# Nine first tiles instead of ten, and a matrix product begun one quarter of k at a time

## The chip, the core and the metric

The kernel runs on one core of a Trainium2 chip. The core has a matrix engine (TensorE, PE in the profile), which multiplies a 128-row stationary operand with a moving operand of up to 512 columns and adds into PSUM banks; a vector engine (VectorE, DVE); a scalar engine (ScalarE, ACT); GpSimd (POOL, almost idle here); and a sync engine (SP), which only issues transfers. Sixteen DMA engines move the data; two queues feed them here, that of SP (q1 in the profile) and that of ACT (q10). PSUM has eight banks of 128 x 512 float32.

The metric is the time of one execution on the device in microseconds (us), where lower is better.

## What is computed

A linear layer whose weight is first pruned 2:4: along the input dimension the 1024 rows of `w` form 256 groups of four, and in every group and column the entries survive whose magnitude is at least the second largest of the four.

```python
B, S, D = 16, 512, 1024            # x: (16, 512, 1024), w: (1024, 1024), b: (1024), all bfloat16
wg  = w.reshape(D // 4, 4, D)
mag = jnp.abs(wg)
thr = second largest of the four magnitudes, per group and column
wp  = (wg * (mag >= thr)).reshape(D, D)
out = jnp.einsum("bsd,df->bsf", x, wp) + b
```

Seen as matrices this is 8192 tokens x 1024 inputs times 1024 inputs x 1024 outputs, with a bias.

## The kernel before

**Tiles.** The tokens form 64 tiles of 128. A tile needs 16 matmuls of 512 columns: eight blocks of 128 inputs (k) times two halves h of the outputs. The weight is pruned on the chip, which takes a while, so the tiles fall into two kinds. The last 54 tiles (t = 10 to 63) are the natural ones: their x is transposed by a DMA transpose on SP's queue, in batches of 2, 4, 8, 8, ... tiles, and each runs its 16 matmuls in a row (line 301) from the finished weight `wp_nat`. The first T = 10 tiles are worked off while the weight is still being pruned, one weight piece at a time.

**Weight pieces.** `w` is cut into two row halves g (512 rows each, k half 0 and 1) and eight pieces: (g=0) columns 0:128, 128:256, 256:512, 512:768, 768:1024, and (g=1) 0:256, 256:512, 512:1024. They are numbered 0 to 7. In the loaded layout partition p holds four consecutive rows m = 0..3, that is one pruning group, so that pruning is elementwise between four slices. For g = 0 the first tiles use this layout directly: x's first half is loaded plainly, transposed on PE against an identity matrix with a stride of four (four transposes per tile, line 160) and copied by ACT to `xT` (line 165). For g = 1 the piece is unpacked into natural row order: four SBUF-to-SBUF transfers j = 0..3, each of 32 partitions, into `wp_nat[h][:, 4 + j]` (line 150); x's second half for the first tiles comes as `xg1` by one DMA transpose (line 98). So transfer j delivers exactly the quarter m = j of k that matmul m of a first tile reads.

**The written order.** A string FRONT gives the order of all work of the first tiles. Each engine and each DMA queue runs its own part strictly in that order; between engines only data, PSUM banks and DMA semaphores make anyone wait. The tokens:

- `W`, `w`: warm-up matmuls on zeros, of 512 and 128 columns (PE).
- `A.i`: magnitudes of piece i (DVE for pieces 0 and 2, ACT for the others); `P.i`: the seven DVE operations that prune it.
- `T.t`, `C.t`: the four transposes of tile t on PE, and their copy on ACT.
- `M.i.t`: the four matmuls of tile t with piece i; `X.q.t`: those of tile t with a whole 512-column quadrant q = 2g + h.
- `V.h.t`: the g = 0 sum of half h is copied from its bank to SBUF in float32 (ACT). `O.h.t`: the g = 1 sum is added to that (DVE). `B.h.t`: the bias is added and the half goes to the output tile (DVE), which is stored when both halves are there.
- `U.g.h.c0.c1`: the four unpacking transfers, issued on SP's queue; `Z` the same on ACT's queue, for the g = 0 half that only natural tiles read.
- `L.n`: the DMA transpose of batch n, on SP's queue, behind the `U`s.

PSUM banks are handed out in turn, eight in a circle, at each `T` and at the first matmul of each quadrant of a tile; the next owner waits for the `V`, `O` or final addition that empties the bank. DMA transfers share eight completion semaphores in turn, so that a transfer's issue can also wait for the transfer that used its semaphore before.

After FRONT come the natural tiles. On DVE they carry along the `B` additions that are left over (three per tile, four in the first). Outputs are stored in pairs of tiles on ACT's queue; tile 62 goes alone, and the last tile, 63, is computed in four column parts so that little is left to do after its last matmul.

**Places the change touches.** `T = 10` (line 39), the load of x for tiles 8 and 9 (line 91), `mm_part` (lines 169 to 179), the batch list (line 224), FRONT (lines 231 to 241) and the pairing of stores (lines 306 to 313).

Of the kernel before, what the change touches and what calls it, by code (L numbers as in the profile page):

```python
# [10 lines left out]
def kernel(  # L11
# [7 lines left out]
    nc = tc.nc  # L19
    P = 128  # L20
# [11 lines left out]
    NT = NTOK // P  # L32
    FH = 512
# [2 lines left out]
    xf = x.flatten_outer_dims()  # L36
    of = out.flatten_outer_dims()

    T = 10
    NE = 8  # L40

    const = ctx.enter_context(tc.tile_pool(name="const", bufs=1))
# [18 lines left out]
    pieces = [(0, 0, 128), (0, 128, 256), (0, 256, 512), (0, 512, 768), (0, 768, 1024),  # L61
              (1, 0, 256), (1, 256, 512), (1, 512, 1024)]
# [25 lines left out]
    load_x(4, 6)  # L88
    load_x(6, 8)
    load_w(0, 512, 1024)  # L90
    load_x(8, 10)
    load_w(1, 0, 512)
    load_w(1, 512, 1024)
    bias_sb = const.tile([P, Dout], bf16, name="bias_sb")
# [12 lines left out]
    def warm(n):  # L107
        K(nc.tensor.matmul(bank[7][:, :n], lhsT=zeros[:, :P], rhs=zeros[:, :n], start=True, stop=True))  # L108
# [3 lines left out]
    def abs_piece(i, on_act):  # L112
        g, c0, c1 = pieces[i]
        n = c1 - c0
        if n <= 256:
            mag = mags_pool.tile([P, 4, n], bf16, name="mag")[:]
        else:
            mag = const.tile([P, 4, n], bf16, name=f"mag_{i}")[:]
        if on_act:
            K(nc.scalar.activation(mag, w_of(i), Act.Abs))  # L120
        else:
            K(nc.vector.tensor_single_scalar(
                mag.bitcast(u16), w_of(i).bitcast(u16), 0x7FFF, op=Alu.bitwise_and))
        mags[i] = mag
# [41 lines left out]
        xT[t] = xt  # L166


    def mm_part(q, t, c0, c1):
        g, h = divmod(q, 2)  # L170
        if c0 == 0 and q > 0:
            own[(q, t)] = next_bank()
        dst = bank[own[(q, t)]][:, c0:c1]
        for m in range(4):
            if g == 0:
                lhs, rhs = xT[t][:, m, :], w_gh[(0, h)][:, m, c0:c1]
            else:
                lhs, rhs = xg1[:, m, t * P:(t + 1) * P], wp_nat[h][:, 4 + m, c0:c1]
            K(nc.tensor.matmul(dst, lhsT=lhs, rhs=rhs, start=c0 == 0 and m == 0, stop=c1 == FH and m == 3))  # L179
# [11 lines left out]
    def to_stage(h, t):  # L191
        stage[(h, t)] = const.tile([P, FH], fp32, name=f"stage{h}_{t}")
        K(nc.scalar.copy(stage[(h, t)][:], bank[own[(h, t)]][:]))  # L193
# [20 lines left out]
    def issue_batch(t0, nb):  # L214
# [6 lines left out]
            xN[t0 + j] = xt[:, :, j * P:(j + 1) * P]  # L221


    batches = [(T, 2), (T + 2, 4)] + [(t, 8) for t in range(T + 6, NT, 8)]

# [1 line left out]


    FRONT = """
        A.0 A.1 P.0 W W W W W W W W w w T.0 T.1 C.0 T.2 T.3 C.1 P.1 w M.0.0 C.2 M.0.1 T.4 C.3 T.5 M.0.2 C.4 T.6 T.7
        A.2 M.0.3 C.5 M.0.4 P.2 M.1.0 M.1.1 C.6 M.0.5 M.1.2 C.7 M.0.6 M.1.3 M.1.4 A.3 M.0.7 M.1.5 M.1.6 M.1.7 A.4
        M.2.0 P.3 M.2.1 V.0.0 M.2.2 V.0.1 M.2.3 T.8 T.9 C.8 M.2.4 M.2.5 C.9 P.4 M.2.6 A.5 M.2.7 X.0.8 V.0.2 X.0.9
        V.0.3 V.0.4 M.3.0 P.5 U.1.0.0.256 V.0.5 M.3.1 M.3.2 V.0.6 M.3.3 V.0.7 M.4.0 M.3.4 A.6 M.3.5 M.4.1 V.0.8 P.6
        U.1.0.256.512 M.4.2 V.0.9 M.3.6 M.4.3 A.7 M.3.7 M.4.4 M.4.5 M.4.6 V.1.0 P.7 U.1.1.0.512 L.0 L.1 L.2 M.4.7
        V.1.1 X.1.8 V.1.2 X.1.9 V.1.3 M.5.0 V.1.4 M.5.1 V.1.5 M.5.2 V.1.6 M.5.3 M.6.0 V.1.7 M.5.4 V.1.8 O.0.0 M.5.5
        M.6.1 V.1.9 Z.0.0.0.512 Z.0.1.0.512 B.0.0 M.5.6 O.0.1 M.5.7 M.6.2 B.0.1 M.6.3 M.6.4 O.0.2 M.6.5 O.0.3 M.6.6
        M.6.7 O.0.4 X.2.8 O.0.5 X.2.9 O.0.6 M.7.0 O.0.7 O.0.8 M.7.1 O.0.9 M.7.2 O.1.0 M.7.3 O.1.1 M.7.4 O.1.2 O.1.3
        M.7.5 O.1.4 M.7.6 O.1.5 M.7.7 O.1.6 X.3.8 B.0.2 O.1.7 X.3.9 O.1.8 O.1.9  # L240
    """
    for tok in FRONT.split():
        k, *n = tok.split(".")
        n = [int(c) for c in n]
        if k in "Ww":
            warm(FH if k == "W" else P)
        elif k == "A":
            abs_piece(n[0], n[0] not in (0, 2))
        elif k == "P":
            prep_piece(n[0])  # L250
        elif k == "T":
            transpose_half(n[0])
        elif k == "C":
            copy_half(n[0])
        elif k == "M":
            g, c0, c1 = pieces[n[0]]
            h = c0 // FH
            mm_part(2 * g + h, n[1], c0 - h * FH, c1 - h * FH)
# [32 lines left out]
    for bi, (t0, nb) in enumerate(batches):  # L291
        if bi >= 1 and bi + 2 < len(batches):
            issue_batch(*batches[bi + 2])
        for t in range(t0, t0 + nb):
            if t == NT - 1:
                last_tile(t)
                continue
            bks = (next_bank(), next_bank())
            for kt in range(KT):
                for h in range(2):  # L300
                    K(nc.tensor.matmul(bank[bks[h]][:], lhsT=xN[t][:, kt, :], rhs=wp_nat[h][:, kt, :],  # L301
                                       start=kt == 0, stop=kt == KT - 1))
# [12 lines left out]
_INS = ['x', 'w', 'b']  # L315
_OUTS = [((16, 512, 1024), 'bfloat16')]
# [25 lines left out]
```

## Time and profile before

| | before |
|---|---|
| time, median of 3 runs | 234.63 us (234.07 to 235.2) |
| the profiled execution: its time | 234.52 us |
| its span, first to last instruction | 232.7 us |
| PE busy | 227.3 us (98%) |
| DVE busy | 117.6 us (51%) |
| ACT busy | 22.7 us (10%) |
| granted TensorE clock, mean | 1.000 |
| DMA, mean over the span | 164 GB/s |

The 1.8 us between the profiled execution's time and its span lie before its first and after its last instruction. A matmul's duration in the profile runs from its start to the modelled end of its result and overlaps its successor: a 512-column matmul has 379 ns there, while the next starts 0.216 us after it; for 256 columns the starts are 0.109 us apart, for 128 columns 0.056 us. What a matmul costs PE is the distance between starts. A few matmul records are missing from the trace; the places show as a "wait" of 0.05 us in the chain of waits, every 50 matmuls.

### The profile page before, as it was taken

To read this page: it belongs to the slowest core of one execution; us is meant where nothing else is said; L and a number is where in the kernel's file an instruction comes from. 1 tells how busy PE (TensorE), PEld (TensorE's weight loads), DVE (VectorE), ACT (ScalarE), POOL (GpSimd) and SP (SyncE) were. 2 spreads that over 40 slices of the span, in tenths; PEclk is the share of its full clock that TensorE was granted. 3 is DMA by queue.
4 is the path that set the end of the run, shared out by engine and by line. 5 is a ranking of instruction groups with operands and counts; after the bars stand their busy time and mean duration, and the time that the engine had idled before them with its cause. 6 is when DMAs were issued, how large, how long until landed. Compare 5 with 4: busy or idle time off the path is not lost.

```text
span 232.7 us, 2893 instructions
## 1 busy us (share of the span) xinstructions
PE 227.3 (98%) x1199; PEld 114.8 (49%) x1219; DVE 117.6 (51%) x209; ACT 22.7 (10%) x38; POOL 0.7 (0%) x6
## 2 busy tenths in 40 slices
PE   7999999999999999999999999999999999999995
PEld 3878774444444444444444444444444444444443
DVE  3999898969375244234334334324424423433434
ACT  3989600000000000000000000000000000000000
POOL 1000000000000000000000000000000000000000
PEclk9999999999999999999999999999999999999999
DMA  6996499999989401993229932597228991122222
GB/s 197 350 211 145 98 197 165 229 315 289 213 215 346 152 24 66 262 236 136 90 44 254 205 130 92 112 218 216 88 90 188 158 250 65 64 93 90 90 90 90
DMA packets 76700, 38.19 MB, mean 164 GB/s; under 512 B 61840, under 2 KB 68496, under 8 KB 76688
## 3 DMA queue, kind: packets, MB, share of 16 engines
q1 hardware_dynamic: 66192, 19.86, 47.1%
q10 hardware_dynamic: 10496, 18.16, 22.4%
q8 instruction: 9, 0.15, 0.3%
q14 instruction: 3, 0.02, 0.0%
HBM read 3.67 MB, written 16.78 MB: 88 GB/s over the span
## 4 chain that ended last, share of the span: by engine, by line
PE 95%; DMA 2%; SPq 1%; issue 1%; DVE 0%
PE bank L301 78%; PE bank L179 15%; DMA xh<-in_x_dram 2%; PE bank L276 2%; PE bank L160 1%; SPq L71 0%; SPq L79 0%; DVE o_sb L286 0%
## 5 line engine op out<-in xcount | busy, mean ns | idle before, releaser
L301 PE MATMUL bank<-wp_nat,xTb 128*128 128x512 bf16 x737 | 161.7, 379 | 0.8
L207 DVE TENSOR_TENSOR o_pair<-bank,bias_sb 128x512 bf16<-128x512 f32 x106 | 68.2, 685 | 98.0 <-PE bank L301 93.6
L301 PEld LDWEIGHTS <-xTb 128*128 128x128 bf16 x752 | 73.6, 98 | 88.7
L301 PE MATMUL bank<-wp_nat,xTs 128*128 128x512 bf16 x94 | 20.8, 379 | 0.1
L179 PE MATMUL bank<-w,xT 128*128 128x256 bf16 (+2 forms) x174 | 18.2, 262 | 0.2
L179 PE MATMUL bank<-wp_nat,xg 128*128 128x256 bf16 (+1 forms) x111 | 17.5, 318 | 0.1
L201 DVE TENSOR_TENSOR o_sb<-stage,bias_sb 128x512 bf16<-128x512 f32 x20 | 13.0, 685 | 7.3 <-DMA out_dram<-o_sb 7.2
L179 PEld LDWEIGHTS <-xT 128*128 128x128 bf16 x176 | 14.5, 98 | 3.1 <-ACT xT L165 0.3
L301 PEld LDWEIGHTS <-xTs 128*128 128x128 bf16 x96 | 9.4, 98 | 11.3
L179 PEld LDWEIGHTS <-xg 128*128 128x128 bf16 x112 | 11.0, 98 | 6.4
L197 DVE TENSOR_TENSOR stage<-bank,stage 128x512 f32<-128x512 f32 x20 | 13.0, 684 | 2.0 <-PE bank L179 1.8
L193 ACT COPY stage<-bank 128x512 f32<-128x512 f32 x20 | 10.3, 681 | 0.3 <-PE bank L179 0.3
L120 ACT ACTIVATE mag<-w 128x1024 bf16<-128x1024 bf16 (+2 forms) x6 | 6.9, 1167 | 0.4 <-DMA w<-in_w_dram 0.4
L142 DVE TENSOR_TENSOR mask<-mag,thr 128x1024 bf16<-128x1024 bf16 (+2 forms) x8 | 5.5, 692 | 0.3
L143 DVE TENSOR_TENSOR w<-w,mask 128x1024 bf16<-128x1024 bf16 (+2 forms) x8 | 5.5, 692 | 0.3
L165 ACT COPY xT<-bank 128x512 bf16<-128x512 bf16 x10 | 5.2, 598 | 1.9 <-PE bank L160 1.9
L108 PE MATMUL bank<-zeros 128*128 128x512 bf16 (+1 forms) x11 | 4.0, 536 | 1.2 <-DVE zeros L101 1.2
L276 PE MATMUL bank<-wp_nat,xTb 128*128 128x128 bf16 (+2 forms) x32 | 3.7, 272 | 0.0
L160 PE MATMUL bank<-ident,xh 128*128 128x128 bf16 x40 | 3.1, 228 | 0.3 <-DMA xh<-in_x_dram 0.3
L133 DVE TENSOR_TENSOR hi<-mag 128x512 bf16<-128x512 bf16 (+2 forms) x8 | 3.4, 420 | 0.1
L134 DVE TENSOR_TENSOR lo<-mag 128x512 bf16<-128x512 bf16 (+2 forms) x8 | 3.3, 417 | 0.0
L276 PEld LDWEIGHTS <-xTb 128*128 128x128 bf16 x32 | 2.5, 98 | 1.3
(16 smaller groups left out, 16.0 us busy)
## 6 DMA issues: line engine op xcount, KB each, us to landing
out_dram<-o_pair ACTq DMA_DIRECT2D x26, 512.0 KB, 2.9
out_dram<-o_sb ACTq DMA_DIRECT2D x10, 256.0 KB, 5.3
w<-in_w_dram SPq DMA_DIRECT2D x3, 512.0 KB, 7.0
xh<-in_x_dram SPq DMA_DIRECT2D x4, 256.0 KB, 4.9
wp_nat<-w ACTq DMA_DIRECT2D x8, 128.0 KB, 4.8
wp_nat<-w SPq DMA_DIRECT2D x8, 64.0 KB, 2.1
wp_nat<-w SPq DMA_DIRECT2D x4, 128.0 KB, 4.5
xh<-in_x_dram ACTq DMA_DIRECT2D x1, 256.0 KB, 4.2
```

Source lines behind the costliest of these rows:

```text
L120: K(nc.scalar.activation(mag, w_of(i), Act.Abs))
L142: K(nc.vector.tensor_tensor(mask, mag, thr[:, None, :].to_broadcast([P, 4, n]), op=Alu.is_ge))
L143: K(nc.vector.tensor_tensor(w_of(i), w_of(i), mask, op=Alu.mult))
L160: K(nc.tensor.transpose(dst[:, m, :], xv[:, m, :], ident[:]))
L165: K(nc.scalar.copy(xt[:], src))
L179: K(nc.tensor.matmul(dst, lhsT=lhs, rhs=rhs, start=c0 == 0 and m == 0, stop=c1 == FH and m == 3))
L193: K(nc.scalar.copy(stage[(h, t)][:], bank[own[(h, t)]][:]))
L197: K(nc.vector.tensor_tensor(st, bank[own[(2 + h, t)]][:], st, op=Alu.add))
L201: K(nc.vector.tensor_tensor(get_o(t)[:, f], stage.pop((h, t))[:], bias_sb[:, f], op=Alu.add))
L207: K(nc.vector.tensor_tensor(o_sb[:, f], bank[bk][:], bias_sb[:, f], op=Alu.add))
L276: K(nc.tensor.matmul(bank[bk][:, :c1 - c0], lhsT=xN[t][:, kt, :], rhs=wp_nat[h][:, kt, c0:c1], start=kt == 0, stop=kt == KT - 1))
L301: K(nc.tensor.matmul(bank[bks[h]][:], lhsT=xN[t][:, kt, :], rhs=wp_nat[h][:, kt, :], start=kt == 0, stop=kt == KT - 1))
```

## The change

T becomes nine. Tile 9 loses its transposes, its copy, its four `X` groups and its `V`, `O` and `B`; it becomes the first natural tile, and the batches are now 3, 4, 8, 8, ... tiles. `mm_part` takes the list of k quarters to multiply, and a new token `N.i.t.m` multiplies one quarter m of tile t with piece i. FRONT begins piece 5 with `N.5.0.0 N.5.1.0 N.5.2.0` (quarter 0 of tiles 0, 1, 2), then quarter 1 of these three tiles, and so on; piece 6 begins with the quarters of tile 0, and piece 7 with those of tiles 0 and 1 in turn. Elsewhere FRONT changes its order: near the start `M.0.2` stands before `T.4` instead of behind `T.5`; `T.8` stands after `V.0.0`; all `B`s move behind FRONT. The `Z`s still follow the last `V`, and that is now `V.1.8`. With an odd number of first tiles the pairs of stored tiles shift by one, and tiles 61 and 62 are stored one by one.

```diff
-    T = 10
+    T = 9
...
-    load_x(8, 10)
+    load_x(8, 9)
...
-    def mm_part(q, t, c0, c1):
+    def mm_part(q, t, c0, c1, ms=range(4)):
         g, h = divmod(q, 2)
-        if c0 == 0 and q > 0:
+        if c0 == 0 and q > 0 and 0 in ms:
             own[(q, t)] = next_bank()
         dst = bank[own[(q, t)]][:, c0:c1]
-        for m in range(4):
+        for m in ms:
...
-    batches = [(T, 2), (T + 2, 4)] + [(t, 8) for t in range(T + 6, NT, 8)]
+    batches = [(T, 12 - T), (12, 4)] + [(t, 8) for t in range(16, NT, 8)]
...
-        A.0 A.1 P.0 W W W W W W W W w w T.0 T.1 C.0 T.2 T.3 C.1 P.1 w M.0.0 C.2 M.0.1 T.4 C.3 T.5 M.0.2 C.4 T.6 T.7
-        A.2 M.0.3 C.5 M.0.4 P.2 M.1.0 M.1.1 C.6 M.0.5 M.1.2 C.7 M.0.6 M.1.3 M.1.4 A.3 M.0.7 M.1.5 M.1.6 M.1.7 A.4
-        M.2.0 P.3 M.2.1 V.0.0 M.2.2 V.0.1 M.2.3 T.8 T.9 C.8 M.2.4 M.2.5 C.9 P.4 M.2.6 A.5 M.2.7 X.0.8 V.0.2 X.0.9
-        V.0.3 V.0.4 M.3.0 P.5 U.1.0.0.256 V.0.5 M.3.1 M.3.2 V.0.6 M.3.3 V.0.7 M.4.0 M.3.4 A.6 M.3.5 M.4.1 V.0.8 P.6
-        U.1.0.256.512 M.4.2 V.0.9 M.3.6 M.4.3 A.7 M.3.7 M.4.4 M.4.5 M.4.6 V.1.0 P.7 U.1.1.0.512 L.0 L.1 L.2 M.4.7
-        V.1.1 X.1.8 V.1.2 X.1.9 V.1.3 M.5.0 V.1.4 M.5.1 V.1.5 M.5.2 V.1.6 M.5.3 M.6.0 V.1.7 M.5.4 V.1.8 O.0.0 M.5.5
-        M.6.1 V.1.9 Z.0.0.0.512 Z.0.1.0.512 B.0.0 M.5.6 O.0.1 M.5.7 M.6.2 B.0.1 M.6.3 M.6.4 O.0.2 M.6.5 O.0.3 M.6.6
-        M.6.7 O.0.4 X.2.8 O.0.5 X.2.9 O.0.6 M.7.0 O.0.7 O.0.8 M.7.1 O.0.9 M.7.2 O.1.0 M.7.3 O.1.1 M.7.4 O.1.2 O.1.3
-        M.7.5 O.1.4 M.7.6 O.1.5 M.7.7 O.1.6 X.3.8 B.0.2 O.1.7 X.3.9 O.1.8 O.1.9
+        A.0 A.1 P.0 W W W W W W W W w w T.0 T.1 C.0 T.2 T.3 P.1 C.1 w M.0.0 C.2 M.0.1 C.3 M.0.2 T.4 A.2 T.5 C.4
+        M.0.3 P.2 T.6 T.7 C.5 M.0.4 M.1.0 C.6 M.1.1 M.0.5 M.1.2 C.7 M.0.6 M.1.3 A.3 M.1.4 M.0.7 M.1.5 M.1.6 A.4
+        M.1.7 P.3 M.2.0 M.2.1 V.0.0 M.2.2 A.5 T.8 M.2.3 M.2.4 C.8 M.2.5 V.0.1 P.4 M.2.6 V.0.2 M.2.7 X.0.8 V.0.3
+        V.0.4 M.3.0 M.3.1 V.0.5 M.3.2 P.5 U.1.0.0.256 V.0.6 M.3.3 V.0.7 M.3.4 M.3.5 A.6 M.3.6 M.4.0 V.0.8 M.4.1
+        V.1.0 P.6 U.1.0.256.512 M.3.7 M.4.2 V.1.1 M.4.3 A.7 M.4.4 M.4.5 M.4.6 M.4.7 V.1.2 P.7 U.1.1.0.512 L.0 L.1
+        L.2 X.1.8 V.1.3 N.5.0.0 N.5.1.0 N.5.2.0 N.5.0.1 N.5.1.1 N.5.2.1 N.5.0.2 N.5.1.2 N.5.2.2 N.5.0.3 N.5.1.3
+        N.5.2.3 V.1.4 V.1.5 V.1.6 M.5.3 M.5.4 V.1.7 M.5.5 V.1.8 Z.0.0.0.512 Z.0.1.0.512 M.5.6 N.6.0.0 N.6.0.1 M.5.7
+        N.6.0.2 N.6.0.3 M.6.1 O.0.0 M.6.2 O.0.1 M.6.3 M.6.4 O.0.2 M.6.5 M.6.6 O.0.3 M.6.7 O.0.4 X.2.8 O.0.5 N.7.0.0
+        N.7.1.0 N.7.0.1 N.7.1.1 N.7.0.2 N.7.1.2 N.7.0.3 N.7.1.3 O.0.6 O.0.7 M.7.2 O.0.8 O.1.0 M.7.3 O.1.1 M.7.4
+        O.1.2 M.7.5 O.1.3 M.7.6 O.1.4 O.1.5 M.7.7 O.1.6 X.3.8 O.1.7 O.1.8
...
+        if k in "MN":
+            g, c0, c1 = pieces[n[0]]
+            h = c0 // FH
+            mm_part(2 * g + h, n[1], c0 - h * FH, c1 - h * FH, n[2:] or range(4))
...
-            if j == 1 or t == NT - 2:
-                dst = of[(t - j) * P:(t + 1) * P, :].rearrange("(j p) f -> p j f", p=P)
-                K(nc.scalar.dma_start(dst, o_pair[:, :j + 1, :]))
+            if j == 1 or t >= NT - 3:
+                j0 = j if t >= NT - 3 else 0
+                dst = of[(t - j + j0) * P:(t + 1) * P, :].rearrange("(j p) f -> p j f", p=P)
+                K(nc.scalar.dma_start(dst, o_pair[:, j0:j + 1, :]))
```

More of the change, by code (lines that the diff above doesn't have):

```diff
@@ L244 @@
         n = [int(c) for c in n]
-        if k in "Ww":
+        if k in "MN":
+            g, c0, c1 = pieces[n[0]]
+            h = c0 // FH
+            mm_part(2 * g + h, n[1], c0 - h * FH, c1 - h * FH, n[2:] or range(4))
+        elif k in "Ww":
             warm(FH if k == "W" else P)
@@ L254 @@
             copy_half(n[0])
[L255 to L258, printed above, removed]
         elif k == "X":
```

## The prediction

> **What bounds the kernel now.** I read the page's busy times first, then the chain of work that ended last, then the order of time on PE, DVE, ACT and SP in the first 44 us, and last the transfers of that stretch. The busy times, and the chain (start us, length us, what):
>
> ```profile
> span 232.7 us, 2893 instructions
> PE 227.3 (98%) x1199; PEld 114.8 (49%) x1219; DVE 117.6 (51%) x209; ACT 22.7 (10%) x38; POOL 0.7 (0%) x6
> ```
> ```profile
> 2.47 4.91 DMA xh<-in_x_dram
> ...
> 13.44 0.45 PE bank L160 x8
> ...
> 33.33 10.09 PE bank L179 x46
> 43.42 1.73 PE bank L301 x8
> ```
>
> After a load of x at the start, the chain is PE alone to 229.95. I compared the start of every matmul with the one before it: from 8.16 on PE never stops. So the end moves only by PE work removed or by a wait that opens on PE. The last waits are early, in PE's order of time (start, length):
>
> ```profile
> 6.26 0.89 PE L179 MATMUL bank<-w,xT 128*128 128x128 bf16 x8
> 7.42 0.64 PE L160 MATMUL bank<-ident,xh 128*128 128x128 bf16 x8 [0.27 <-DMA xh<-in_x_dram]
> ```
>
> How much later may the inputs of the first tiles come? These rows set them:
>
> ```profile
> 19.75 10.34 SPq L150 DMA_DIRECT2D wp_nat<-w  x12
> ...
> 22.18 4.58 ACT L193 COPY stage<-bank 128x512 f32<-128x512 f32 x9
> ...
> 26.12 0.64 ACTq L150 DMA_DIRECT2D wp_nat<-w  x1
> 26.20 1.22 DVE L143 TENSOR_TENSOR w<-w,mask 128x2048 bf16<-128x2048 bf16 x1
> ```
>
> The last line ends the pruning of piece 7 at 27.42; DVE worked on pruning without a pause from 3.72 to there. The first is SP's twelve unpacking issues; those of piece 7 start at 27.45, 28.04, 28.70 and 29.35. The middle two are ACT's copies and, behind them, its first `Z`. The transfer issues alone in two short windows are the third and fourth quarters of piece 7 (KB, us to landing):
>
> ```profile
> wp_nat<-w SPq DMA_DIRECT2D x1, 128.0 KB, 5.7
> ```
> ```profile
> wp_nat<-w SPq DMA_DIRECT2D x1, 128.0 KB, 5.9
> ```
>
> So the quarters landed at 30.33, 31.43, 34.37 and 35.23. `M.7.0` began at 34.63 and read its fourth quarter at 34.63 + 3 x 0.216 = 35.27: the kernel before runs with 0.04 us to spare there. That is the place to watch.
>
> **The change part by part.**
>
> *Removed PE work.* Tile 9's four transposes. The chain has eight (T.8 and T.9) in 0.45 us: 0.22 us off. Its 16 matmuls of 512 columns only move to line 301 at the same 0.216 us. Splitting by quarters keeps the number and width of matmuls: nothing.
>
> *The new start.* Before, PE sat from 6.99 to 7.42 for x of tile 4. `M.0.2` now fits in: the copy C.2 ends at 6.583 + 0.605 = 7.19, with 0.055 to PE it starts at 7.24, ends at 7.47, and T.4 follows. T.5 ends at 7.91, `M.0.3` fills to 8.13, T.6 starts with its x (landed 8.11) as before, T.7 ends at 8.63 as before, but one tile part (4 x 0.056) more is done: 0.22 us. C.4 moves 0.02 later and ends at 8.48, in time for `M.0.4` at 8.63.
>
> *Sum if nothing waits: -0.45 us.* Now each cover, walked along PE with the rows' durations:
> - `T.8` at 12.62 needs `V.0.0` (starts 11.95, takes 0.585, 0.055 to PE): 12.59. Covered, by 0.03.
> - ACT goes `V.0.0`, `A.5` at 12.43, `C.8` at 13.39, `V.0.1` to `V.0.7` every 0.477, `A.6` at 17.2 (P.6 needs it at 19.6). X.0.8 starts at 15.03, `M.3.0` at 15.89 instead of 17.20. Every bank is emptied over 1 us before its next owner.
> - `A.7` follows `V.1.1`, which needs `M.4.1` (ends 19.98): 20.49 instead of 20.37, done 22.49. Piece 7's pruning began at 22.49: at most 0.05 later, and its unpacking too.
> - `X.1.8` ends, and `N.5.0.0` starts, at 25.91 - 0.45 - 2 x 0.863 = 23.74. Piece 5 landed at 21.86, 22.54, 23.18 and 25.13, the last 1.3 late (3.4 us against 2.1 of its three siblings). Quarter 3 is wanted at 24.72. Bounds: nothing, or 25.18 - 24.72 = 0.46. Piece 6 (25.30 to 27.23) is wanted from 26.80, its last quarter at 27.56: nothing, or, with the `Z`s beside it, some 0.3.
> - `N.7.0.0` starts at 31.59, 3.04 before `M.7.0` did (0.45, and three quadrants of tile 9). Quarters 0 and 1 (30.33, 31.43) are there at 31.59 and 32.02. Quarter 2 is wanted at 32.45, quarter 3 at 32.88. Two tiles per quarter buy 0.43 per quarter; 3.04 were given away.
>
> *What the last two quarters do.* Lower bound: alone, the `Z`s of this size took 2.6 to 2.7; 29.40 + 2.7 = 32.1, no wait. Upper bound, landings as before: quarter 2 waits 34.42 - 32.45 = 1.97, two matmuls end at 34.85, quarter 3 waits 35.28 - 34.85 = 0.43: 2.4 us. Between the two stands the neighbour. The `Z`s move too: ACT's backlog after `A.7` is seven `V`s (22.30 + 6 x 0.477 = 25.16) instead of ten, and the first `Z` was issued 0.34 before the last `V`'s start, so at 24.82, 1.3 earlier. Over 28.9 to 33.2 both queues together moved this:
>
> ```profile
> DMA packets 1035, 0.94 MB, mean 220 GB/s; under 512 B 113, under 2 KB 1035, under 8 KB 1035
> ...
> q1 hardware_dynamic: 550, 0.51, 53.2%
> q10 hardware_dynamic: 485, 0.44, 36.0%
> ```
>
> By 28.9 the `Z`s will have some 0.45 of their 1.05 MB done (0.1 beside piece 6 to 27.2, then 1.7 us at the 193 GB/s that they had alone) instead of 0.24. About 0.6 MB are left, as much as piece 7's 0.52: shared evenly at 220, piece 7 is through at 33.6 and lands 0.34 later, 33.95; quarter 2 at about 32.8. That is 0.4 + 0.7 = 1.1 us of waits. In the run before one DMA engine of the sixteen was 1.2 to 1.5 us behind the others at the landings of 34.37 and 35.23 (their fifteenth receipts: 33.12 and 33.72). I take a third of that, a fourth quarter at 34.35: waits of 1.45 us. Earlier waits at pieces 5 and 6 are swallowed by this one, since the later landing does not move.
>
> *Behind it.* DVE has 18 `B`s in the natural tiles (5 x 0.61 us per tile, under 3.45 of PE). Bank 4 for tile 9 waits for `O.1.1`, long done. The stores at the end are smaller and earlier; tile 63 is unchanged: nothing, and if the extra store did delay the last, the cover gone would be some 0.4 us of issue.
>
> **Sum:** -0.45 + 1.45 = +1.0 us against the profiled execution's own 234.52, so 235.5; the median of the runs shown is 234.63, 0.1 above that execution.
>
> **A rule weighed.** The Trainium skill, "DMA: Bandwidth & Descriptors", section on the anatomy of one DMA, fits a transfer (on the software path, not measured for this one) as 2.0 us plus bytes over 436 GB/s. That agrees with the 2.1 us of a 64 KB piece alone; for 128 KB it gives 2.3, an estimate by that page of 31.7 for the fourth quarter, and so the first rival's time. The 5.9 us row speaks against it wherever the other queue is full.
>
> **The rivals.**
> 1. *The unpacking lands in time* because the `Z`s, 1.3 us earlier, are out of its way: quarter 3 by 32.9. Time 234.52 - 0.45 = 234.1 (up to 234.5 with the 0.46 of piece 5). For it: 2.7 us alone, and `Z`s that no longer wait for piece 7's semaphore (one was issued at 31.45, behind the landing of 31.43). Against: at 28.9 some 1.1 MB are left, which at 220 GB/s takes until 33.9.
> 2. *The first natural batch is late*, slower than before. Its transfer now has three tiles. Two took 10.2 us, from 30.35 to 40.55; the third is 0.26 MB, 0.9 us at the 290 GB/s that DMA transposes reached alone (40.5 to 43), 2.9 at the 90 that they had beside the `Z`s. Landing 41.5 to 43.4; tile 9 is wanted at 39.4, with my waits at 40.8. It decides from a landing of 40.9 on: time +1.7 to +3.6, 236.2 to 238. For it: the `Z`s would have to end at 39 to 40 again. Against: issued 1.3 earlier and unhindered, they are through by 34, and three tiles at 290 then land by 38.
> 3. *The clock falls* when PE pauses for over a microsecond: the warm-up matmuls before 4.6 us have starts 0.427 apart for 512 columns. 3.4 us at that rate add 1.7: 237.2. Against: after the pause of 0.4 before 7.42 the rate was full. The Trainium skill, "TensorE: Matmul & The Clock Gate", Part 1, puts the idle window at about 3.4 us, longer than my longest wait; no run here shows it.
>
> **How the numbers follow.** About 0.5% (1.2 us) is what a measurement of this kernel can tell from no change; its own runs spread that far. My forecast, the late last quarters, 0.62: +0.1 to +2.0, time 234.6 to 236.5, about 0.37 of it within 0.5% and 0.25 beyond. Rival 1: 0.18, within 0.5%. Rival 2: 0.14, slower. Rival 3: 0.03, slower. Something that I don't see, faster by over 0.5%: 0.03. Together faster 0.03, same 0.55, slower 0.42. The range leaves out most of rival 2 and rival 3: 234.0 to 236.9. The forecast's own range is 234.6 to 236.5.
>
> **What would show it.** Right: PE gaps before the third and fourth quarter's matmuls of piece 7, at 32 to 35 us, of 0.7 to 2.4 together; `M.0.2` before 7.42; the first `Z` near 24.8; 36 transposes; no gap from tile 9 on. Wrong: no gap at piece 7 (rival 1), a gap before the first line-301 matmul (rival 2), or a `V`, `O` or `A.7` that releases PE late.

## The result

| | before | changed |
|---|---|---|
| median, runs taken side by side | 235.13 us (9 runs, 234.07 to 235.37) | 236.14 us (9 runs, 235.32 to 236.66) |
| profiled execution, its span | 234.52 us, 232.7 us | 236.37 us, 234.6 us |

The ratio is 1.0055, 95% interval 1.0035 to 1.0074: slower by about half a per cent. Between the medians it is 1.0 us (0.43%), between the averages 1.3 us. A second measurement on another chip (below) gave 1.0064. The profiled execution of the changed kernel is 1.85 us longer than the one before, so it shows more loss than the median.

The profile page of the changed kernel (busy us, share, count; for the groups: busy us and mean ns, then the idle time before them and what ended it):

```profile
span 234.6 us, 2876 instructions
PE 227.3 (97%) x1194; PEld 114.5 (49%) x1215; DVE 116.6 (50%) x207; ACT 21.3 (9%) x35; POOL 0.7 (0%) x6
...
L179 PE MATMUL bank<-wp_nat,xg 128*128 128x256 bf16 (+1 forms) x103 | 16.1, 313 | 1.6 <-DMA wp_nat<-w 1.5
...
L160 PE MATMUL bank<-ident,xh 128*128 128x128 bf16 x36 | 2.8, 222 | 0.3 <-ACT stage L193 0.3
```

Four transposes are gone (36 are left), PE is busy just as long, and the span is longer: time went into waits, 1.5 us of them on the unpacked weight. PE's order of time (start, length, in brackets the idle time before) says where:

```profile
13.17 11.06 PE L179 MATMUL bank<-w,xT 128*128 128x256 bf16 x90
24.06 1.15 PE L179 MATMUL bank<-wp_nat,xg 128*128 128x256 bf16 x9
26.10 3.06 PE L179 MATMUL bank<-wp_nat,xg 128*128 128x256 bf16 x26 [0.89 <-DMA wp_nat<-w]
29.78 11.96 PE L179 MATMUL bank<-wp_nat,xg 128*128 128x256 bf16 x68 [0.62 <-DMA wp_nat<-w]
41.58 5.78 PE L302 MATMUL bank<-wp_nat,xTs 128*128 128x512 bf16 x25
```

Nine matmuls of piece 5 run (quarters 0 to 2 of three tiles) and PE stands until the fourth quarter lands at 26.06. The second wait is before the last quarter of piece 6. Then there is none: the 68 matmuls of the fifth line run through all of piece 7, and tile 9 follows at 41.58. The brackets count from the modelled end of the matmul before; by the distance between starts, less the normal pitch, the waits are 1.05 and 0.85 us. From here on "wait" means that distance.

The account up to tile 9 closes. Of the kernel before, PE's order of time shows `T.6`, the stretch with the unpacked weight, and tile 10:

```profile
8.15 0.64 PE L160 MATMUL bank<-ident,xh 128*128 128x128 bf16 x8
...
25.91 17.51 PE L179 MATMUL bank<-wp_nat,xg 128*128 128x256 bf16 x111
43.26 4.05 PE L301 MATMUL bank<-wp_nat,xTs 128*128 128x512 bf16 x17
```

Tile 10 started at 43.26 there, so the start of tile 9 would answer to 39.81 (less 16 x 0.216); now it is 41.58, 1.77 later. Waits: 1.05 + 0.85, and two earlier ones, 0.27 before `M.2.0` and 0.42 before `T.8`: 2.59. Less the forecast gain of 0.45, and less some 0.35 because x landed about that much earlier in this execution (for `T.6` at 7.75 instead of 8.11): 1.79. In this and the other profiles the span ends 192.9 to 193.1 us after that start, so the start of tile 9 is a good measure of what a version is worth.

Where does the fourth quarter of piece 5 lose its time? Its issue stands alone in a window of 22.2 to 22.7 us (KB, us to landing), and a window of 23.3 to 25 us holds one packet on a queue that the kernel does not use (packets, MB, share of 16 engines):

```profile
wp_nat<-w SPq DMA_DIRECT2D x1, 64.0 KB, 3.9
```
```profile
q8 instruction: 1, 0.02, 5.5%
```

The packet is 16 KB of instructions for PE. It started at 23.46 and took 1.51 us, until 24.97. A transfer gives one receipt for each of the sixteen DMA engines: fifteen of the quarter's were there at 24.25, the last at 26.05. Before, such a packet ran from 22.76 to 24.03, and the quarter, alone in the window from 21.75 to 22.25 us, landed late as well:

```profile
wp_nat<-w SPq DMA_DIRECT2D x1, 64.0 KB, 3.4
```

That the packet is what held the last engine is tested below. The chain of waits of the changed kernel (start, length) shows the next loss, on SP's queue:

```profile
23.04 0.54 SPq L150
...
23.63 1.74 SPq L150
...
25.41 0.60 SPq L150
...
26.06 3.68 DMA wp_nat<-w
...
29.78 3.54 PE bank L179 x30
```

The second issue of piece 6 held SP for 1.74 us (a normal one takes 0.6), and the fourth quarter, issued at 26.06, took 3.68 beside the `Z`s. Before, the four landed between 25.30 and 27.23; now at 26.25, 27.17, 28.85 and 29.74.

### The profile page after: what moved, and what is told of

Its sections match the earlier page's. It is cut to its first block, busy times and chain, and to the rows that moved or that the text cites. A ratio compares the mean times of both kernels' runs of the same rounds, so it can differ in the third digit from the quotient of the medians.

```text
span 234.6 us, 2876 instructions
## 1 busy us (share of the span) xinstructions
PE 227.3 (97%) x1194; PEld 114.5 (49%) x1215; DVE 116.6 (50%) x207; ACT 21.3 (9%) x35; POOL 0.7 (0%) x6
## 4 chain that ended last, share of the span: by engine, by line
PE 75%; DMA 12%; DVE 7%; SPq 2%; issue 1%; ACT 0%; DVEq 0%; ACTq 0%
PE bank L302 69%; DMA out_dram<-o_sb 8%; PE bank L179 5%; DMA w<-in_w_dram 3%; DVE o_sb L201 2%; DMA wp_nat<-w 2%; PE bank L277 1%; SPq L150 1%; DVE mask L142 1%; DVE w L143 1%; SPq L79 1%; DVE hi L133 1%; DVE lo L134 1%; DVE thr L140 1%; SPq L71 0%
## 5 line engine op out<-in xcount | busy, mean ns | idle before, releaser
L207 DVE TENSOR_TENSOR o_pair<-bank,bias_sb 128x512 bf16<-128x512 f32 x108 | 69.5, 686 | 101.7 <-PE bank L302 97.2
L302 PE MATMUL bank<-wp_nat,xTs 128*128 128x512 bf16 x109 | 24.0, 379 | 0.1
L179 PE MATMUL bank<-wp_nat,xg 128*128 128x256 bf16 (+1 forms) x103 | 16.1, 313 | 1.6 <-DMA wp_nat<-w 1.5
L302 PEld LDWEIGHTS <-xTs 128*128 128x128 bf16 x112 | 11.0, 98 | 13.2
L179 PE MATMUL bank<-w,xT 128*128 128x256 bf16 (+2 forms) x166 | 16.7, 256 | 0.4
L179 PEld LDWEIGHTS <-xT 128*128 128x128 bf16 x168 | 13.8, 98 | 2.5 <-ACT xT L165 0.3
L201 DVE TENSOR_TENSOR o_sb<-stage,bias_sb 128x512 bf16<-128x512 f32 x18 | 11.5, 687 | 4.9 <-DMA out_dram<-o_sb 4.9
L179 PEld LDWEIGHTS <-xg 128*128 128x128 bf16 x104 | 10.1, 98 | 7.4 <-issue 1.9
L197 DVE TENSOR_TENSOR stage<-bank,stage 128x512 f32<-128x512 f32 x18 | 11.5, 687 | 3.1 <-PE bank L179 3.1
L193 ACT COPY stage<-bank 128x512 f32<-128x512 f32 x18 | 9.3, 622 | 0.7 <-PE bank L179 0.7
```

Source lines behind the costliest of these rows:

```text
L197: K(nc.vector.tensor_tensor(st, bank[own[(2 + h, t)]][:], st, op=Alu.add))
L201: K(nc.vector.tensor_tensor(get_o(t)[:, f], stage.pop((h, t))[:], bias_sb[:, f], op=Alu.add))
L207: K(nc.vector.tensor_tensor(o_sb[:, f], bank[bk][:], bias_sb[:, f], op=Alu.add))
```

## The experiments

The table puts the runs side by side. "Fetch" is the start of PE's 16 KB instruction packet in this stretch; "piece 5" the time from issue to landing of its last quarter; "waits" those of PE before the last quarters of pieces 5, 6 and 7; "tile 9" its start, for ten first tiles the start of tile 10 less 3.45; "work" the time from the start of `T.6` to that, less all waits of PE in between. The two versions with early `Z`s stand apart, further down.

| version | fetch | piece 5 | waits 5 / 6 / 7 | tile 9 | work | ratio to before, interval |
|---|---|---|---|---|---|---|
| before | 22.76 | 3.4 | 0 / 0 / 0 | 39.81 | 31.65 | 1 |
| changed | 23.46 | 3.9 | 1.05 / 0.85 / 0 | 41.58 | 31.19 | 1.0055, 1.0035 to 1.0074 |
| changed, again | 23.01 | 3.7 | 0.60 / 0.37 / 0.50 | 41.03 | 31.19 | 1.0064, 1.0041 to 1.0087 |
| more warm-ups | 19.73 | 2.1 | 0 / 0.84 / 0.53 | 40.54 | 31.19 | 1.0048, 1.0032 to 1.0064 |
| `Z` held back | 23.65 | 4.0 | 1.09 / 0 / 0 | 42.03 | 31.19 | 1.0118, 1.0097 to 1.0139 |
| no quarters | 22.69 | 3.6 | 1.26 / 0.09 / 0.83 | 41.34 | 31.18 | 1.0082, 1.0059 to 1.0104 |
| old order, nine | 23.16 | 3.4 | 1.20 / 1.29 / 0.34 | 42.23 | 31.39 | 1.0140, 1.0086 to 1.0194 |
| quarters, ten | 22.80 | 3.2 | 0 / 0 / 0 | 39.55 | 31.65 | 1.0002, 0.9993 to 1.0012 |
| new start, ten | 23.21 | 3.5 | 0 / 0 / 0 | 39.87 | 31.40 | 0.9989, 0.9974 to 1.0004 |
| one queue, nine | 19.98 | 2.1 | 0 / 0 / 0.06 | 40.45 | 31.17 | 1.0031, 1.0019 to 1.0043 |
| small first batch, nine | 19.99 | 2.1 | 0 / 0 / 0 | 39.34 | 31.20 | 0.9997, 0.9987 to 1.0007 |
| one queue, ten | 20.14 | 2.1 | 0 / 0 / 0 | 39.67 | 31.42 | 1.0012, 0.9995 to 1.0030 |

**The changed kernel once more.**

> The changed kernel once more, for a second profile and to stand beside the others on one chip. Ratio 1.0035 to 1.0074 as measured. Theory 1 (what decides is the landing of the last quarters, pieces 5 to 7, each pushing the next): the waits at pieces 5, 6 and 7 together are 1.5 to 2.3 us again, however they are shared out; the wait of 0.42 us for T.8 and the late load of piece 3 (10.34 against 9.62) need not come back.

Measured: 235.85 us, ratio 1.0064, and PE's order of time is this:

```profile
25.53 3.00 PE L179 MATMUL bank<-wp_nat,xg 128*128 128x256 bf16 x26 [0.44 <-DMA wp_nat<-w]
28.74 5.48 PE L179 MATMUL bank<-wp_nat,xg 128*128 128x256 bf16 x38 [0.21 <-DMA wp_nat<-w]
34.56 6.63 PE L179 MATMUL bank<-wp_nat,xg 128*128 128x512 bf16 x30 [0.33 <-DMA wp_nat<-w]
41.03 6.21 PE L302 MATMUL bank<-wp_nat,xTs 128*128 128x512 bf16 x27
```

The same kernel waits at piece 7 here, for a quarter that landed at 34.52 (34.66 in the first profile, where PE was late enough to want it only at 35.1). The places share the loss out differently from one execution to the next; 1.47 us at the three pieces here (just under the 1.5 to 2.3 expected), 1.90 there. The wait before `T.8` is absent here. In the first profile the weights of piece 3 had landed at 10.34, and `A.3` began at 10.42 (before: 9.62 and 9.79); that set the pruning back by 0.45 and used up the 0.03 of cover.

**More warm-ups.** Eight long warm-ups become 32 short ones: 48 more instructions on PE (24 matmuls and their weight loads), so that the fetch comes at another time. They last as long (32 x 0.107 us against 8 x 0.427), and nothing of the real work changes.

```diff
-        A.0 A.1 P.0 W W W W W W W W w w T.0 T.1 ...
+        A.0 A.1 P.0 w w w w w w w w w w w w w w w w w w w w w w w w w w w w w w w w w w T.0 T.1 ...
```

> The changed kernel with the 8 warm-up matmuls of 512 columns replaced by 32 of 128 columns: the same time on PE, 48 more PE instructions. Theory 1 (the fetch of PE's instructions, a packet of 16 KB that held one DMA engine from 23.5 us for 1.5 us, made the fourth quarter of piece 5 land at 26.06 and held up SP's issues of piece 6): the fetch comes some 24 matmuls earlier, near 21 us, where quarters 0 and 1 have slack; the fourth quarter lands by 24.8, the PE wait of 1.05 us at piece 5 falls under 0.2, and piece 6 lands about 1 us earlier. Theory 2 (the quarter is late for another reason): it lands at 25.5 or later again. On the time: 0.5 to 1.3 us less than the changed kernel's 1.0 us above the kernel before, unless a wait of as much opens at piece 7 (theory 3, the cover that tile 9 gave stands behind all of it): then no change.

Measured: 235.79 us, 1.0048. The fetch came at 19.73, earlier than the 21 expected. Of this kernel: the fetch in a window of 19.5 to 20.9 us, piece 5's fourth quarter in one of 21.97 to 22.5 us, and PE's order of time:

```profile
q8 instruction: 1, 0.02, 5.1%
```
```profile
wp_nat<-w SPq DMA_DIRECT2D x1, 64.0 KB, 2.1
```
```profile
23.55 3.98 PE L179 MATMUL bank<-wp_nat,xg 128*128 128x256 bf16 x35
28.21 5.49 PE L179 MATMUL bank<-wp_nat,xg 128*128 128x256 bf16 x38 [0.68 <-DMA wp_nat<-w]
34.06 6.63 PE L179 MATMUL bank<-wp_nat,xg 128*128 128x512 bf16 x30 [0.36 <-DMA wp_nat<-w]
40.54 6.64 PE L302 MATMUL bank<-wp_nat,xTs 128*128 128x512 bf16 x29
```

The quarter takes 2.1 us, as its undisturbed siblings do, and the wait at piece 5 is gone: the fetch was its cause. The table bears this out. In the eight profiles whose packet started at 22.7 to 23.7 the quarter landed 1.0 to 1.2 us after the packet's end; in the four with the early fetch it took 2.1 us. The waits at pieces 6 and 7 stay, and the time hardly moves, since PE only comes earlier to the next late quarter.

**`Z` held back.** A small copy on ACT reads the bank that holds tile 0's sums of pieces 5 and 6. It waits for the last quarter of piece 6 there, and the `Z`s stand behind it on ACT's queue.

```diff
-        N.5.2.3 V.1.4 V.1.5 V.1.6 M.5.3 M.5.4 V.1.7 M.5.5 V.1.8 Z.0.0.0.512 Z.0.1.0.512 M.5.6 N.6.0.0 N.6.0.1 M.5.7
-        N.6.0.2 N.6.0.3 M.6.1 O.0.0
...
+        N.5.2.3 V.1.4 V.1.5 V.1.6 M.5.3 M.5.4 V.1.7 M.5.5 V.1.8 M.5.6 N.6.0.0 N.6.0.1 M.5.7
+        N.6.0.2 N.6.0.3 G.2.0 Z.0.0.0.512 Z.0.1.0.512 M.6.1 O.0.0
...
+        K(nc.scalar.copy(g_sb[:], bank[own[(q, t)]][:, :16]))
```

> The changed kernel with the unpacking of the other half (the Z transfers on ACT's queue) held back by a small ACT copy that waits for tile 0's sum of pieces 5 and 6. Theory 1 (the Z transfers, issued from 24.3, share the DMA engines with piece 6 and make its last quarter land at 29.74): piece 6 lands by 28.5 and the PE wait of 0.79 us before its last quarter falls under 0.3, while the 1.05 us at piece 5 stay. Piece 7 or the first natural batch then has the Z transfers beside it and may land later. Theory 2 (piece 6 is late because SP's issues are late): it still lands at 29 or later. Time: between 0.8 us less than the changed kernel and 1 us more, by which the first natural tile (wanted near 41) has its inputs or not.

Measured: 237.4 us, 1.0118. PE's order of time, and the issue of the first natural batch (SP's only one in the window from 30.05 to 30.3 us):

```profile
25.74 14.80 PE L179 MATMUL bank<-wp_nat,xg 128*128 128x256 bf16 x94 [0.92 <-DMA wp_nat<-w]
42.03 5.14 PE L308 MATMUL bank<-wp_nat,xTs 128*128 128x512 bf16 x22 [1.50 <-DMA xTs<-in_x_dram]
```
```profile
xTs<-in_x_dram SPq DMA_TRANSPOSE x1, 11.9
```

Without the `Z`s piece 6's last quarter takes 2.1 us instead of 3.7 and lands at 27.15, piece 7's at 33.51, and PE waits for neither. SP was also held for less here (1.12 us), so that this quarter was issued a microsecond earlier, at 25.04. A pair without the hold in this place settles it: with more warm-ups the quarter took 3.6 us beside the `Z`s and PE waited 0.84; with all unpacking on one queue (below) it took 2.1 and PE did not wait. So the `Z`s were the cause at piece 6. The price is a wait of 1.66 us before tile 9, for a batch that landed at 41.99. That is the second rival of the prediction, in a kernel made for something else. The wait at piece 5, where the fetch is (23.65), stays. By the ratios the kernel is 1.5 us behind the changed one, more than the 1 us expected at most.

**No quarters.** Nine tiles and the new order, but whole pieces instead of quarters.

```diff
-        ... N.5.0.0 N.5.1.0 N.5.2.0 N.5.0.1 N.5.1.1 N.5.2.1 N.5.0.2 N.5.1.2 N.5.2.2 N.5.0.3 N.5.1.3 N.5.2.3
+        ... M.5.0 M.5.1 M.5.2
...
-        ... N.6.0.0 N.6.0.1 M.5.7 N.6.0.2 N.6.0.3
+        ... M.6.0 M.5.7
...
-        ... N.7.0.0 N.7.1.0 N.7.0.1 N.7.1.1 N.7.0.2 N.7.1.2 N.7.0.3 N.7.1.3
+        ... M.7.0 M.7.1
```

> The changed kernel without the quarter-by-quarter order: whole four-matmul groups for pieces 5, 6 and 7. Theory 1 (the quarters hide part of a wait): with a fourth quarter at 26.06, PE waits from about 24.4, 1.65 us instead of 1.05, but the wait at piece 6 shrinks by as much, since the landing of its last quarter decides: no change of the time within 0.3 us. Theory 2 (the quarters are worth their 0.6 us): 0.6 us slower than the changed kernel.

Measured: 236.61 us, 1.0082. Tile 0 meets the late quarter of piece 5 after three matmuls and waits 1.26; piece 7 costs 0.83. The interval, 1.0059 to 1.0104, overlaps those of the changed kernel: the quarters may be worth some 0.4 to 0.6 us with nine tiles, or nothing; these runs do not settle it.

**Nine tiles in the old order.** The FRONT of before without tile 9's tokens.

```diff
-        M.2.0 P.3 M.2.1 V.0.0 M.2.2 V.0.1 M.2.3 T.8 T.9 C.8 M.2.4 M.2.5 C.9 P.4 M.2.6 A.5 M.2.7 X.0.8 V.0.2 X.0.9
+        M.2.0 P.3 M.2.1 V.0.0 M.2.2 V.0.1 M.2.3 T.8 C.8 M.2.4 M.2.5 P.4 M.2.6 A.5 M.2.7 X.0.8 V.0.2
```

> Nine first tiles with the order of the kernel before, tile 9's tokens left out, whole groups at pieces 5 to 7. Theory 1 (nine tiles give too little cover, whatever the order): waits of 1.5 to 3 us in all at pieces 5, 6 and 7, 0.5 to 2 us slower than the kernel before. Theory 2 (the new order is at fault, through A.5 before T.8 and the earlier Z transfers): within 0.3 us of the kernel before.

Measured: 237.55 us, 1.0140, with waits of 1.20, 1.29 and 0.34, tile 9 at 42.23. The waits are in the range expected, the time is beyond it. So giving up tile 9 without a new order costs 1.4% (0.9 to 1.9; four runs, one of them at 239.8 us, and 1.2% by the medians). The `Z`s stand behind fewer `V`s here and were issued from 24.00 on, before from 26.12; their share in the loss is part of the 1.4. Order and quarters together win back about 0.8 of these points; the intervals of the two versions all but touch, so how much it is stays open.

**Quarters with ten tiles, and the new start with ten tiles.** Two parts of the change alone on the kernel before: `N.5` to `N.7` as in the change, and `M.0.2` before `T.4`.

```diff
-        ... V.1.3 M.5.0 V.1.4 M.5.1 V.1.5 M.5.2 V.1.6 M.5.3 M.6.0
+        ... V.1.3 V.1.4 N.5.0.0 N.5.1.0 N.5.2.0 N.5.0.1 N.5.1.1 N.5.2.1 N.5.0.2 N.5.1.2 N.5.2.2 N.5.0.3 N.5.1.3 N.5.2.3 V.1.5 V.1.6 M.5.3 N.6.0.0 N.6.0.1 N.6.0.2 N.6.0.3
```

> The kernel before with the quarter-by-quarter order of pieces 5, 6 and 7 alone (three, one and two tiles, as in the change; V.1.4 stays ahead of it). The same matmuls, and no wait to hide in the profile of before: ratio 0.999 to 1.001. With theory 2 of e6 (waits at piece 7 in many runs): 0.1 to 0.4 us faster.

```diff
-        ... M.0.0 C.2 M.0.1 T.4 C.3 T.5 M.0.2 C.4 T.6 T.7
-        A.2 M.0.3 C.5 M.0.4 ...
+        ... M.0.0 C.2 M.0.1 C.3 M.0.2 T.4 T.5 C.4 M.0.3 T.6 T.7
+        A.2 C.5 M.0.4 ...
```

> The kernel before with the start of the changed order alone: M.0.2 before T.4 and M.0.3 before T.6. By the prediction's step 0.22 us of PE time are won, that is ratio 0.999, if the pruning chain on DVE and piece 7 (0.04 us to spare in the profile of before) let it through; if the landing of piece 7 sets the end in most runs, ratio 1.000 and a wait of 0.1 to 0.3 us at M.7.0 in the profile.

Measured: 1.0002 (0.9993 to 1.0012) for the quarters, 0.9989 (0.9974 to 1.0004) for the new start. With ten tiles nobody waits for a quarter, so splitting is worth nothing, and it costs nothing: the work is 31.65 us as before. The new start did not come out of the noise of the times. Its work is 0.25 us shorter, but in this profile x landed late at the very start (5.38 instead of 4.97), so that `T.6` began only 0.46 us behind its own x; the new order had little waiting left to fill there.

**`Z` early, on GpSimd's queue, with nine and with ten tiles.** Both disturbers away at once: the warm-ups as above (nine tiles only), and the `Z`s moved from behind the last `V` to 11.3 and 17.5 us, right behind the pruning of their pieces.

```diff
-        M.1.7 P.3 M.2.0 ...
+        M.1.7 P.3 Z.0.0.0.512 M.2.0 ...
-        V.0.4 M.3.0 M.3.1 V.0.5 M.3.2 P.5 U.1.0.0.256 ...
+        V.0.4 M.3.0 M.3.1 V.0.5 M.3.2 P.5 Z.0.1.0.512 U.1.0.0.256 ...
...
-            unpack(*n, nc.sync if k == "U" else nc.scalar)
+            unpack(*n, nc.sync if k == "U" else nc.gpsimd)
```

> The changed kernel with both disturbers taken away: 32 narrow warm-up matmuls as in e1_more_warmups (earlier fetch), and the Z transfers on GpSimd's queue, issued as soon as pieces 2 and 4 are pruned (11.2 and 16.9 us) instead of behind the last V. Theory 1 (nine tiles give enough cover once pieces 6 and 7 have the DMA engines to themselves): no PE wait over 0.1 us at pieces 5, 6, 7 and at the first natural tile; PE's work is 0.45 us shorter than before, so 0.3 to 0.6 us faster than the kernel before (ratio 0.9975 to 0.9987). Theory 2 (the cover itself is too thin: pruning ends at 27.4, and the last quarter needs 2.6 more after its issue at 29.4): a wait of up to 0.3 us stays at piece 7: ratio 0.999 to 1.001. Theory 3 (the early Z transfers collide with the DMA transpose of x's second half, wanted at 23.7): a wait at piece 5's first quarter, slower than the kernel before.

> The kernel before (ten tiles, its own order) with the Z transfers early on GpSimd's queue. It had no PE wait from 8.2 us on, so there is nothing to gain: ratio 0.999 to 1.001 if its profile stands for its runs. If its runs usually do have waits at piece 7 (0.04 us to spare in the profile; its runs spread over 1.3 us), 0.2 to 0.6 us faster and less spread.

Measured: 239.49 us, 1.0224 (1.0195 to 1.0252) with nine, 241.15 us, 1.0273 (1.0243 to 1.0303) with ten. The transpose of x's second half ran beside the early `Z`s. It is alone in a window of 8 to 8.5 us of the run with nine; before, it took 12.3 us:

```profile
xg<-in_x_dram SPq DMA_TRANSPOSE x1, 18.0
```

The first `Z`s took 12 us instead of 2.6, and piece 5 landed only from 28.3 on. PE stood for 4.5 us (6.0 with ten tiles). The view by stretches of the run with nine (us; busy time of PE, PEld, DVE, ACT, POOL; granted clock, DMA share, GB/s) shows what this cost on top:

```profile
23.90:28.40 4.50, 0.23 (x2) 0.00 (x0) 3.77 (x6) 2.20 (x5) 0.00 (x0) 1.00 0.89 240
28.50:32.60 4.10, 4.10 (x23) 2.99 (x24) 0.00 (x0) 0.00 (x0) 0.00 (x0) 0.59 0.59 129
32.60:41.00 8.40, 8.35 (x60) 5.80 (x59) 6.73 (x12) 0.00 (x0) 0.00 (x0) 1.00 1.12 238
```

After the pause the granted clock is 0.59 for 4.1 us, about 1.7 us lost (4.1 x 0.41). So this pair says nothing on whether nine tiles could win. It shows a worse place for the `Z`s. They changed their queue as well as their time, and the pair does not tell the two apart.

**All unpacking on SP's queue, nine tiles.** The warm-ups as above, and each `Z` as a `U` behind the piece that frees it, so that nothing runs beside pieces 6 and 7.

```diff
-        V.1.0 P.6 U.1.0.256.512 M.3.7 ... V.1.2 P.7 U.1.1.0.512 L.0 L.1
+        V.1.0 P.6 U.1.0.256.512 U.0.0.0.512 M.3.7 ... V.1.2 P.7 U.1.1.0.512 U.0.1.0.512 L.0 L.1
...
-        ... M.5.5 V.1.8 Z.0.0.0.512 Z.0.1.0.512 M.5.6 ...
+        ... M.5.5 V.1.8 M.5.6 ...
```

> The changed kernel with the narrow warm-up matmuls of e1_more_warmups and with all unpacking on SP's queue in the order of need: piece 5, piece 6, the first half of the Z transfers, piece 7, the second half, then the natural batches. Nothing on ACT's queue shares the DMA engines with pieces 5 to 7. Theory 1 (the waits come from sharing the engines with the Z transfers; alone a 128 KB quarter lands 2.7 us after its issue): no wait at pieces 5 and 6, piece 7's last quarter issued near 30.3 and landed near 33.0, a wait of at most 0.3 us; ratio 0.998 to 1.000. Theory 2 (the ten-tile cover can't be replaced): the second half of the Z transfers and the first natural batch, issued 5.2 us later by SP, land after 39.4 and PE waits there for 1 to 3 us; ratio 1.003 to 1.010.

Measured: 235.23 us, 1.0031 (1.0019 to 1.0043). PE's and SP's order of time:

```profile
23.81 15.83 PE L179 MATMUL bank<-wp_nat,xg 128*128 128x256 bf16 x104
40.45 6.86 PE L302 MATMUL bank<-wp_nat,xTs 128*128 128x512 bf16 x31 [0.81 <-DMA xTs<-in_x_dram]
```
```profile
19.93 13.60 SPq L150 DMA_DIRECT2D wp_nat<-w  x20
33.57 8.17 SPq L219 DMA_TRANSPOSE xTs<-in_x_dram  x2
```

All 104 matmuls of the three pieces run without a stop (0.06 us at piece 7, whose last quarter landed at 32.97). But SP issues the first natural batch only behind twenty unpacking transfers, at 33.58. It landed at 40.41, and PE waited 0.97 us for it.

**The same with a first batch of one tile.**

```diff
-    batches = [(T, 12 - T), (12, 4)] + [(t, 8) for t in range(16, NT, 8)]
+    batches = [(T, 1), (T + 1, 11 - T), (12, 4)] + [(t, 8) for t in range(16, NT, 8)]
...
-        L.2 X.1.8 V.1.3 ...
+        L.2 L.3 X.1.8 V.1.3 ...
...
-        if bi >= 1 and bi + 2 < len(batches):
+        if bi >= 2 and bi + 2 < len(batches):
```

> e9_nine_one_queue with the first natural batch of three tiles split into one and two, so that tile 9's x comes first. Theory 1 (the 0.97 us before tile 9 was the landing of its batch, 40.41, set by the batch's size and its late issue at 33.6): the one-tile batch lands by 38.5, PE does not wait before tile 9, the next two tiles are wanted at 42.9: 0.9 us less than e9, ratio 0.998 to 1.000. Theory 2 (the DMA transposes land together whatever their size, since the engines are shared with the one behind): the landing stays near 40, ratio 1.002 to 1.004.

Measured: 234.36 us beside 234.45 of before, 0.9997 (0.9987 to 1.0007). The issue of the one-tile batch (window from 33.4 to 34 us) and PE's order of time:

```profile
xTs<-in_x_dram SPq DMA_TRANSPOSE x1, 4.1
```
```profile
23.72 15.78 PE L179 MATMUL bank<-wp_nat,xg 128*128 128x256 bf16 x104
39.34 7.93 PE L302 MATMUL bank<-wp_nat,xTs 128*128 128x512 bf16 x36
```

Here nothing stops PE at pieces 5, 6, 7 or at tile 9 (0.16 us before `T.8` is all), which starts at 39.34, 0.47 before the kernel before. Just that is what the prediction's first rival asks for. Here x landed 0.18 us earlier than before (at 7.93 for `T.6`), and the wait before `T.8` took 0.16 back, so that 0.45 are the change's own. The span is 232.4 us against 232.7 of the profile before: from the start of the last matmul to the end 3.17 us pass instead of 3.01 (3.06 to 3.09 in the other profiles with nine tiles); why is not shown. The medians are 0.09 apart, and the interval holds both no change and a gain of 0.3 us.

**The same with ten tiles** (the new start, the warm-ups, all unpacking on SP):

```diff
-        U.1.0.256.512 M.4.2 V.0.9 ... P.7 U.1.1.0.512 L.0 L.1 L.2 M.4.7
+        U.1.0.256.512 U.0.0.0.512 M.4.2 V.0.9 ... P.7 U.1.1.0.512 U.0.1.0.512 L.0 L.1 L.2 M.4.7
```

> Ten first tiles with the new start of e10_ten_new_start, the narrow warm-up matmuls and all unpacking on SP's queue as in e9. PE has no wait to lose at pieces 5 and 6, and piece 7's last quarter lands near 33.0 instead of 34.3 to 35.2: 1.5 us to spare. If some runs of the kernel before wait at piece 7, ratio 0.997 to 0.999; if not, that of e10, 0.999.

Measured: 234.5 us, 1.0012 (0.9995 to 1.0030), no waits; neither of the two ratios expected, though the interval does not rule out no change. Ten tiles have cover enough with two queues; one queue gives them nothing. `T.6` began with its x in this profile, and the work is 31.42: the new start's 0.22 is there.

## Why the prediction was right or wrong

**The size: right.** +1.0 us was forecast against the profiled execution's 234.52; the medians are 1.01 apart. The time itself, 236.14, is 0.6 above the 235.5 forecast, because the kernel before came out that much longer in these runs, too (235.13). Both profiled executions of the changed kernel are longer than 235.5 (236.37 and 235.86), inside the forecast's own range of 234.6 to 236.5.

**The gains: right as far as they can be seen.** 36 transposes; `M.0.2` ran at 6.83, before `T.4` at 7.08, as PE's order of time of the changed kernel shows, twelve matmuls of tiles 0 to 2 in one line ahead of the transposes:

```profile
6.05 1.17 PE L179 MATMUL bank<-w,xT 128*128 128x128 bf16 x12
7.08 0.64 PE L160 MATMUL bank<-ident,xh 128*128 128x128 bf16 x8
...
7.80 0.64 PE L160 MATMUL bank<-ident,xh 128*128 128x128 bf16 x8
```

The last line is `T.6`, which starts 0.05 us after its x has landed, as it does before (0.04). So the work from there to tile 9 tells the gain: 31.65 us before, 31.17 to 31.20 in all versions with nine tiles and the new start, 31.39 with nine tiles in the old order, 31.40 and 31.42 with ten tiles and the new start. That is 0.45 to 0.48 for both parts, 0.26 for tile 9's transposes and 0.23 to 0.25 for the start; 0.22 was forecast for each. In the medians the gain was never seen.

**The mechanism: right in kind.** Tile 9's cover is given up, and the last quarters of unpacked pieces come too late. The old order with nine tiles shows what is lost with tile 9 when nothing else is done, 1.4%. The place was wrong in the first profile: of the gaps that were to show the forecast right, at 32 to 35 us, there is none.

**The step that failed: "Earlier waits at pieces 5 and 6 are swallowed by this one, since the later landing does not move."** In the first profile it was the reverse: the waits at 5 and 6 (1.90 us) swallowed that at 7, of which 1.45 were forecast. In the second, all three were there, 0.60, 0.37 and 0.50. The forecast for piece 7's landing itself was good (34.35; 34.66 and 34.52 measured). What was wrong was how late PE would come to it, because two bounds were too low:
- Piece 5, "nothing, or 0.46": 1.05 and 0.60. The row was there (the last quarter took 3.4 us against 2.1), but it was taken as a given delay at a given place. It is a collision of that transfer with PE's fetch of instructions, and how late it lands depends on when the packet ends: 3.2 to 4.0 us after the issue in the versions of the table whose fetch fell at 22.7 to 23.7.
- Piece 6, "some 0.3": 0.85 and 0.37. Two things were left out: SP's issue itself was held (1.74 us instead of 0.6, 1.25 in the run before), and the `Z`s, first issued at 24.27 (24.82 was forecast), were under way before any of its quarters had landed.

The two errors came out alike in sum, 1.45 forecast against 1.90 and 1.47. That the total fits is in part because the three waits stand in for one another, and in part luck: the wait that the sum was built on, 1.45 at piece 7, measured nothing in one execution and 0.50 in the other.

**`T.8`'s cover of 0.03** held in the second profile and failed by 0.42 in the first, with a late load of weights. A cover that small should have had a bound of its own. The 0.27 before `M.2.0` stood in no list of covers: the pruning of piece 2 ended at 11.16 as before, and PE, with x 0.35 earlier and 0.22 gained, was there first.

**Rival 1** (in time) needs both disturbers away and a quicker first batch: the one-tile batch with a single queue is that kernel, and it equals the one before. **Rival 2** (first natural batch late) did not occur in the changed kernel, where it landed at 40.03 and PE came at 41.58. It occurs as soon as the quarters come in time (41.99 and 40.41). **Rival 3** (clock) was rightly small. The view by stretches of the changed kernel over the first wait, same columns as above:

```profile
24.90:26.20 1.30, 0.41 (x4) 0.22 (x3) 1.24 (x2) 1.30 (x3) 0.00 (x0) 1.00 0.42 70
```

The clock stays at 1.00; after the 4.5 us pause with the `Z`s moved early it was 0.59. By the Trainium skill, "TensorE: Matmul & The Clock Gate", Part 1, the gate falls to half after an idle window of about 3.4 us; both rows agree.

**The rule that was weighed.** The fourth quarter of piece 7 in the changed kernel, SP's only issue in the window from 30.2 to 30.7 us:

```profile
wp_nat<-w SPq DMA_DIRECT2D x1, 128.0 KB, 4.6
```

With the `Z`s on the other queue it took 4.6 us; in the version with nine tiles and all unpacking on one queue transfers of this size took 2.5 to 3.0. The Trainium skill's "DMA: Bandwidth & Descriptors", section on the anatomy of one DMA, fits the software path with 2.0 us plus bytes over 436 GB/s, an estimate of 2.3 us here: near the row without a neighbour, and half of the row with one.

## What to carry to other kernels

Before you give up work that covers a transfer, count for each part of that transfer when it lands and when it will be wanted, with the slowest landing that any run shows. A transfer over sixteen engines lands with its slowest engine (above: fifteen receipts at 24.25, the last at 26.05). Where several late landings lie in a row, removing one only uncovers the next: here the fetch, then the neighbour's transfers, then the next batch had to go before the 0.45 us showed in the trace, and it was too small for the medians.

## What was not expected of the hardware

- **PE's own instructions cost data transfers time.** The changed kernel fetched nine packets of 16 KB for 2409 recorded PE instructions, about one per 256. In the stretch looked at here a packet took 0.9 to 1.5 us, and a quarter of piece 5 that met it landed 1.0 to 1.8 us late; shifting the fetch by 48 instructions removed this. With the early fetch the packet meets the first two quarters instead, which land 0.2 to 0.6 us late, where there is slack. The Trainium skill, "Runtime: NRT & Kernel Launch", section on instruction fetch mechanics, gives blocks of 16 KiB or 256 instructions, which agrees, and calls the cost of crossing one mostly hidden. For PE's own work that agrees, too: in the kernel before PE never stops from 8.16 us on. The cost came by way of a transfer.
- **The packet holds an issue of SP, too.** In the twelve profiles of the table one unpacking issue of SP near the packet takes 0.9 to 1.7 us instead of 0.6, and it ends 0.2 to 0.4 us after the packet does. With the early fetch the hold moves along, from piece 6 to the second issue of piece 5 (0.95 us with more warm-ups). By what path the packet holds the issue, no run shows.
- **Copies beside a DMA transpose slow both.** With early `Z`s the 128 KB SBUF-to-SBUF copies on GpSimd's queue took 8.0 to 12.5 us beside it with nine tiles, and the transpose 18.0 instead of 12.3. It is not that queue alone: on ACT's queue six of the held-back `Z`s, issued beside the first natural batch, took 7.2 to 9.1 us, where 2.6 was the time of one alone.
- **A chain line need not be a wait of PE.** The chain of the changed kernel gives 8% to stores of `out_dram<-o_sb` from 43 to 65 us, through DVE's `B`s; PE's starts have no gap there.
